# A recurrence and a two-layer network in one kernel: 20 of 24 chunks computed in pairs of two batches on 64x64 parts of the array

## The chip, the cores and the metric

The kernel runs on one core of one Trainium2 chip. Its engines are TensorE (PE in the profile, with PEld for its weight loads), VectorE (DVE), ScalarE (ACT), GpSimd (POOL) and SyncE (SP), which issues nearly all DMAs. The metric is the device time of one execution in microseconds, as a median of several runs; lower is better.

## The reference

`r`, `k`, `v`, `w` have the shape (batch 4, heads 8, tokens 768, 48). For every batch and head a 48x48 state is carried over the tokens, and the result of all heads of a token, 384 numbers, goes through two matrices with a leaky ReLU between them:

```python
for t in range(S):
    cur = einsum('bhd,bhe->bhde', u[None] * k_t, v_t)
    y[:, :, t] = einsum('bhd,bhde->bhe', r_t, state + cur)
    state = w_t[:, :, :, None] * state + einsum('bhd,bhe->bhde', k_t, v_t)
x = y.transpose(0, 2, 1, 3).reshape(B * S, H * D)     # 3072 x 384
h = x @ w_in                                          # 384 x 2048
out = maximum(0.01 * h, h) @ w_out                    # 2048 x 384
```

All inputs and the output are float32.

## The kernel before, in words

The tokens are cut into chunks of 128, six to a batch, 24 in all. Within a chunk the recurrence is written as matrix products: with L the running sum of ln w, `r*exp(L)` and `k*exp(-L)` are formed, transposed, and multiplied into scores of 128x128 tokens per head; the scores are masked to earlier tokens and multiplied with v (L829, "intra"); r times the state that came in is added (L824, "inter"); the state is brought forward with k and v (L798, "sums"). The part of the token itself, with u, is made on GpSimd and VectorE ("bonus", L435 to L447) and added to y (L478). y is transposed into `xT` and feeds the network: "up" (L901) multiplies with w_in into a PSUM tile `hp`, ScalarE applies Prelu (L916) into `g`, "down" (L928) multiplies with w_out into `op`, the result is copied (L939, L941) and stored (L945).

Chunks are done in the order `seq`. The first four come as two calls of `pair`: each takes 256 tokens of one batch, two neighbouring tokens to a partition (index j), and multiplies on parts of the array: its scores (L624) on 64x64 parts, its state sums (L583) and its intra product (L649) on 64x128 parts. The other 20 go through `single`, one chunk of 128 tokens at a time with the full array, except that the scores (L858) use 48 rows of two row halves for the two heads of a pair. `run` puts the scores of two chunks into one step for the chunks in MERGED. The transposes of r and k go over TensorE (L416) or, for chunks in RK_DMA, by a DMA transpose on SP's queue (L764); those of y over TensorE (L464) or, for Y_DMA, by a DMA transpose (L843).

The order of all work is made by `Plan`. Every step has a cost for each engine that may run it, a priority, the steps that it depends on and the buffers that it takes. `order` is a list scheduler over these costs: whenever an engine is free it takes the ready step with the lowest priority number whose buffers are free. Attention steps have ten times the chunk's number, ups and downs 1000 and more, so attention goes first and the network fills in. The instructions are then issued in that order, and each engine keeps it: an instruction that waits holds up all behind it on its engine. RANK and FORCE move priorities of the first 144 steps and fix the engine of some; SLACK adds a reserve to the planned end of steps from priority 50 on, LATE to DMAs. LEAD and AHEAD tie the first step (Ln) and the loads of a chunk to earlier chunks. `blocks` says how many chunks go through the network together. All PSUM tiles, eight of 512 columns, are one pool `ps`, with limits by kind (two `hp`, two `op`, one `cp`, one `ek`, two `yy`). Until 24 us gaps on TensorE are filled with products of zeros (L970).

Of the kernel before, what the change touches and what calls it, by code (L numbers as in the profile page):

```python
# [15 lines left out]
class Buf:  # L16


    def __init__(self, pool, kind=None):
        self.pool, self.kind, self.users, self.t, self.free_at = pool, kind or pool, [], None, 0.0  # L20


class Plan:
# [7 lines left out]
    def __init__(self, limits, slack_from, slack, late):  # L31
        self.steps, self.limits, self.late = [], limits, late
        self.slack_from, self.slack = slack_from, slack
# [8 lines left out]
    def order(self, pools):  # L42
# [10 lines left out]
        remain = {k: len(b.users) for k, b in bufs.items()}  # L53
        free_tiles = {p: [(0.0, k) for k in range(len(t))] for p, t in pools.items()}
        in_use = {}
        ready_at = [0.0] * n
        self.start, self.done, self.eng = [None] * n, [0.0] * n, [None] * n
# [15 lines left out]
        while events:  # L73
# [13 lines left out]
            for e in self.ENGINES:  # L87
# [3 lines left out]
                while ready[e]:  # L91
# [3 lines left out]
                    want, ok = {}, True  # L95
                    for b in self.steps[i][5]:
                        if b.t is None:
                            want[b.pool] = want.get(b.pool, 0) + 1
                            if in_use.get(b.kind, 0) >= self.limits.get(b.kind, 99):
                                ok = False  # L100
                    for p, k in want.items():
                        if sum(f <= now + 1e-9 for f, _ in free_tiles[p]) < k:
                            ok = False
# [10 lines left out]
                for b in takes:  # L114
                    if b.t is None:
                        slots = free_tiles[b.pool]
                        s = min(slots)
                        slots.remove(s)
                        b.slot = s[1]
                        b.t = pools[b.pool][s[1]]  # L120
                        in_use[b.kind] = in_use.get(b.kind, 0) + 1
                d = engs[e]
                self.start[i], self.eng[i] = now, e
# [7 lines left out]
                else:  # L131
# [5 lines left out]
                    self.done[i] = dma_free + lat + (self.late if now > 20 else 0.0)  # L137
                heapq.heappush(events, (free[e], 1, e, -1))
# [5 lines left out]
                for b in {id(b): b for b in (*reads, *takes)}.values():  # L144
                    b.free_at = max(b.free_at, self.done[i])
                    remain[id(b)] -= sum(u == i for u in b.users)
                    if remain[id(b)] == 0:
                        free_tiles[b.pool].append((b.free_at, b.slot))
# [7 lines left out]
BOTH = (1.5, 64, 1.45, 0.2)  # L156
WEIGHT = (2.08, 24, 2.6, 0.2)
# [4 lines left out]
RANK = {0: 15.37, 1: 14.4, 2: 3.33, 3: 23.03, 4: 38.76, 5: 12.01, 6: -26.8, 7: -21.87, 8: -21.96, 9: -19.05,  # L162
# [22 lines left out]
def kernel(  # L185
# [91 lines left out]
    with tc.manual_schedule():  # L277
# [10 lines left out]
        for t in pools["lw"]:  # L288
            nc.vector.memset(t[:, :, D:64], 0.0)
# [715 lines left out]
```

## Time and profile before

| | us |
|---|---|
| median of 3 runs (lowest to highest) | 182.65 (181.78 to 183.76) |
| the profiled execution, its own time | 181.38 |
| its span, first to last instruction | 179.6 |
| TensorE busy | 171.6 (2036 matmuls) |
| VectorE, ScalarE, GpSimd busy | 115.0, 115.3, 102.5 |
| up (L901), 720 matmuls, busy | 73.3 |
| down (L928), 384 matmuls, busy | 73.4 |
| first up | at 19.0 |

The granted clock of TensorE is 0.996 of full speed over the span. In lines of groups the columns are: line, engine, operation, what is written and read, shapes, count, then busy us and mean ns of one, then the idle time ahead. In lines of a timeline: start, us from the first start to the last end of the group, engine, line, what, count. Matmuls overlap, so the time that a group holds TensorE is read from its start to the start of the next group, not from the mean. In lines of waits: who waited for whom, us in total, how often, the longest.

### The profile page before, as it was taken

Reading aid. Unit: us, or ns where it says so; the run is one execution under the profiler, and the core shown is the slowest. Engines: PE = TensorE matmul, PEld = TensorE weight load, DVE = VectorE, ACT = ScalarE, POOL = GpSimd, SP = SyncE. Lnnn points to the kernel's source line nnn. Section 1 sums busy time; section 2 is a strip of 40 time slices with the busy share of each in tenths; the row PEclk is TensorE's granted clock in tenths of the full one; section 3 lists DMA queues with packets and bytes.
Section 4 is the critical chain, followed back from the end, with each engine's and each line's share of the span. In section 5 each row is a group of like instructions: output and inputs, shape, how many; then the busy total and the mean of one; then the engine's idle time right before and its main releaser. Section 6 shows DMA issues by size and latency. Waiting matters only on the chain.

```text
span 179.6 us, 5197 instructions
## 1 busy us (share of the span) xinstructions
PE 171.6 (96%) x2036; PEld 129.8 (72%) x2037; DVE 115.0 (64%) x231; ACT 115.3 (64%) x253; POOL 102.5 (57%) x138
## 2 busy tenths in 40 slices
PE   7798999999999999999999999999999999999991
PEld 2466888867778788877788767787788786787850
DVE  7699764289789898559677558397468297241102
ACT  2678968855867788884489774485486664652610
POOL 5999632574897686877469854667165665100000
PEclk9999999999999999999999999999999999999998
DMA  5999999998999999999999989999899996600112
GB/s 141 261 283 316 370 376 364 187 199 199 231 191 224 180 229 134 184 213 173 185 181 223 212 179 223 153 215 175 152 254 170 220 163 134 167 9 19 47 44 88
DMA packets 116571, 34.43 MB, mean 192 GB/s; under 512 B 109121, under 2 KB 115778, under 8 KB 116546
## 3 DMA queue, kind: packets, MB, share of 16 engines
q1 hardware_dynamic: 116544, 34.09, 95.8%
q8 instruction: 16, 0.26, 0.7%
q14 instruction: 9, 0.07, 0.1%
q10 hardware_dynamic: 2, 0.00, 0.0%
HBM read 25.17 MB, written 4.72 MB: 166 GB/s over the span
## 4 chain that ended last, share of the span: by engine, by line
PE 77%; DMA 11%; DVE 4%; ACT 2%; issue 2%; SPq 1%; POOL 0%; DVEq 0%; ACTq 0%
PE ps L901 35%; PE ps L928 28%; DMA in<-in_r_dram 3%; DMA in<-in_v_dram 3%; DMA in<-in_w_dram 2%; PE ps L858 2%; DMA xT<-y 2%; PE ps L829 2%; PE ps L717 2%; PE ps L824 2%; PE ps L416 2%; DVE rk L405 2%; PE ps L798 1%; PE ps L464 1%; DVE m L636 1%
## 5 line engine op out<-in xcount | busy, mean ns | idle before, releaser
L901 PE MATMUL ps<-xT,w_in_b 128*128 128x256 bf16 (+1 forms) x720 | 73.3, 251 | 0.4 <-ACT xT L471 0.2
L928 PE MATMUL ps<-w_out_b,g 128*128 128x384 bf16 x384 | 73.4, 326 | 0.0
L916 ACT ACTIVATE g<-ps 128x512 bf16<-128x512 f32 x96 | 56.8, 597 | 25.4 <-PE ps L901 23.2
L901 PEld LDWEIGHTS <-w_in_b 128*128 128x128 bf16 x720 | 57.8, 98 | 9.9 <-issue 0.7
L928 PEld LDWEIGHTS <-g 128*128 128x128 bf16 x384 | 35.2, 98 | 17.3
L405 DVE TENSOR_TENSOR rk<-in,ps 128x384 bf16<-128x384 f32 x46 | 24.5, 548 | 9.9 <-ACT ps L743 6.5
L435 POOL TENSOR_TENSOR ru<-in,ub 128x384 f32<-128x384 f32 x24 | 23.9, 1001 | 9.6 <-DMA in<-in_k_dram 7.6
L788 DVE TENSOR_TENSOR m<-ps,maskb 128x512 bf16<-128x512 f32 x40 | 25.1, 683 | 5.3 <-PE ps L858 5.3
L439 POOL TENSOR_TENSOR ru<-ru,in 128x384 f32<-128x384 f32 x24 | 24.6, 1027 | 3.0 <-DMA in<-in_r_dram 2.4
L775 POOL TENSOR_TENSOR sb<-s,a 128x384 bf16<-128x384 f32 x18 | 15.0, 831 | 16.8 <-ACT a L738 16.8
L447 POOL TENSOR_TENSOR vs<-in,dg 128x384 f32<-128x384 f32 x20 | 16.6, 830 | 9.1 <-DVE dg L443 8.4
L729 DVE TENSOR_TENSOR ci<-ps,lw 128x384 f32<-128x384 f32 x20 | 11.1, 555 | 9.7 <-PE ps L720 4.5
L939 DVE COPY o<-ps 128x384 f32<-128x384 f32 x10 | 5.6, 555 | 15.6 <-PE ps L928 15.4
L443 DVE TENSOR_REDUCE dg<-ru 128x8 f32<-128x384 f32 x24 | 12.9, 544 | 2.1 <-POOL ru L439 2.1
L478 DVE TENSOR_TENSOR y<-ps,vs 128x384 bf16<-128x384 f32 x20 | 11.1, 553 | 3.2 <-PE ps L829 2.6
L455 POOL CAST vb<-in 128x384 bf16<-128x384 f32 x24 | 12.0, 504 | 1.5 <-DMA in<-in_v_dram 1.4
L711 ACT ACTIVATE lw<-in 128x384 bf16<-128x384 f32 x20 | 10.4, 522 | 2.9 <-DMA in<-in_w_dram 2.9
L743 ACT ACTIVATE ps<-ps 128x384 f32<-128x384 f32 x20 | 9.6, 481 | 4.1 <-DVE ci L729 3.6
L738 ACT ACTIVATE a<-ps 64x4 f32<-64x4 f32 x36 | 6.0, 167 | 7.7 <-DVE ci L729 5.1
L813 DVE TENSOR_TENSOR s<-ps,sb 128x384 f32<-128x384 f32 x14 | 7.7, 552 | 3.8 <-PE ps L798 2.7
L747 ACT ACTIVATE ps<-ci 128x384 f32<-128x384 f32 x20 | 9.8, 491 | 0.0
L941 ACT COPY o<-ps 128x384 f32<-128x384 f32 x14 | 6.7, 479 | 4.2 <-PE ps L928 4.0
(90 smaller groups left out, 176.2 us busy)
## 6 DMA issues: line engine op xcount, KB each, us to landing
out_dram<-o SPq DMA_DIRECT2D x24, 192.0 KB, 3.7
in<-in_w_dram SPq DMA_DIRECT2D x20, 192.0 KB, 4.2
in<-in_k_dram SPq DMA_DIRECT2D x20, 192.0 KB, 4.2
in<-in_r_dram SPq DMA_DIRECT2D x20, 192.0 KB, 4.0
in<-in_v_dram SPq DMA_DIRECT2D x20, 192.0 KB, 4.0
in<-in_moe_w_out_dram SPq DMA_DIRECT2D x4, 768.0 KB, 12.1
in<-in_moe_w_in_dram SPq DMA_DIRECT2D x4, 384.0 KB, 6.8
in<-in_moe_w_in_dram SPq DMA_DIRECT2D x2, 768.0 KB, 9.0
```

Source lines behind the costliest of these rows:

```text
L405: (nc.gpsimd if e == "POOL" else nc.vector).tensor_tensor(out=o, in0=x, in1=i, op=ALU.mult)
L435: lambda e: nc.gpsimd.tensor_tensor(out=ru.t[:], in0=kv(), in1=ubv, op=ALU.mult),
L439: lambda e: nc.gpsimd.tensor_tensor(out=ru.t[:], in0=ru.t[:], in1=rv(), op=ALU.mult),
L443: lambda e: nc.vector.tensor_reduce(out=dg.t[:], in_=ru.t[:], axis=AX.X, op=ALU.add),
L447: lambda e: nc.gpsimd.tensor_tensor(out=vs.t[:], in0=vv(), in1=dg.t[:].unsqueeze(2).to_broadcast([128, H, D]), op=ALU.mult),
L455: {"POOL": 0.56}, lambda e: nc.gpsimd.tensor_copy(out=vb.t[:], in_=vv()),
L478: lambda e: nc.vector.tensor_tensor(out=y.t[:], in0=heads(yp.t), in1=vs.t[:], op=ALU.add),
L775: lambda e: nc.gpsimd.tensor_tensor(out=sb.t[:].rearrange("p g a d -> p (g a) d"), in0=s_in.t[:].rearrange("p g a d -> p (g a) d"), in1=a_ ...
L788: lambda e, par=par: nc.vector.tensor_tensor(out=m.t[:, par, :, :], in0=sc[par].t[:].rearrange("p (g t) -> p g t", g=NP), in1=maskb[:].uns ...
L901: nc.tensor.matmul(hp.t[:, a * N : (a + 1) * N], lhsT=w_in_b[:, t, (j + a) * 128 : (j + a + 1) * 128], rhs=xT[:, t, c0 : c0 + N], start=(a ...
L916: lambda e, hp=hp, g=g, j=j, J=J, N=N: nc.scalar.activation(out=g.t[:, j : j + J, 0:N], in_=hp.t[:, 0 : J * N].rearrange("p (a n) -> p a n ...
L928: nc.tensor.matmul(op.t[:, 0:DM], lhsT=g.t[:, j, off : off + 128], rhs=w_out_b[:, j, :], start=(j == 0), stop=(j == NJ - 1))
```

## The change

`single` and `run` go; `late(n)` takes their place and treats chunks n and n+1 together, which are now the same 128 tokens of two batches b and b+1. Batch x sits on partitions 64x to 64x+63, with two neighbouring tokens (j) to a partition. A load moves 64 partitions with 96 floats in a row. Each of the scores, the inter and the intra product and the state sums is then a set of matmuls on 64x64 parts: a row half for the batch or the head's parity, a column half for the batch, the token parity or the head's parity. They are laid in two rows on TensorE: first half of inter and the scores (`row(behind, scores)`), and, after the masks, the other half of inter, intra and the sums (`row(ahead, intra, sums)`). The state holds head pairs as 128x192 instead of 128x384. `seq` is arranged in pairs of batches.

With it: ci is two VectorE subtractions and additions from one cumulative sum; a bonus product `vs` is written in 64-partition pieces (four a pair); the last of the r products in `pair` (tokens of the first parity) may go to GpSimd (cost 1.15 on VectorE, 1.0 on GpSimd) and stands there in the program's order for both pairs; a new mask `maskp` is made by eight selects on GpSimd at the start, and maskb goes. Prelu puts the tokens back in order by reading PSUM with a stride. The last chunk's down is cut into columns 0 to 255 and 256 to 383. The up steps of one-chunk blocks wait for all of the w_in columns that they read. `blocks` has eight single chunks (six before). The planner also holds off a step whose PSUM tile is still in use by the other side, and can hand out neighbouring tiles together. RANK and FORCE are empty, LEAD is 5, AHEAD 3, SLACK 0, LATE 0.6; DMA transposes now carry a pair, for r and k 16 blocks instead of 8, for y 6 instead of 3. `pair` is split into part lists, of which only the whole one is used, and its state is kept in two halves of 64 partitions.

Instructions in program order: matmuls 2037 before, 3106 after, of which on 64x64 parts 64 and 1568; GpSimd selects 8 and 15; vs 20 and 40; loads in the late chunks 80 and 80; DMA transposes 21 and 16.

```diff
-RANK = {0: 15.37, 1: 14.4, ...
-FORCE = {23: "DVE", 26: "DVE", ...
+RANK = {}
+FORCE = {}
-    RK_DMA = {6, 11, 12, 14, 15, 16, 17, 18, 19, 20, 21, 22, 23}
-    Y_DMA = {8, 10, 16, 17, 20, 21, 22, 23}
-    MERGED = {6, 10, 12, 14, 16, 18, 20}
-    LEAD = 4
-    AHEAD = 4
-    SLACK_FROM = 50
-    SLACK = 0.2
-    LATE = 0.0
+    RK_DMA = {8, 10, 12, 14, 16, 18, 20, 22}
+    Y_DMA = {8, 10, 12, 14, 16, 18, 20, 22}
+    LIMITS = {"hp": 2, "op": 2, "cp": 1, "ek": 3, "yy": 2, "warm": 1, "warm2": 1}
+    LAST = [(0, 256), (256, DM)]
+    LEAD = 5
+    AHEAD = 3
+    SLACK_FROM = 60
+    SLACK = 0.0
+    LATE = 0.6
-    blocks = [2, 1, 1, 1, 1, 2, 2, 2, 2, 2, 1, 1, 2, 2, 2]
+    blocks = [1, 1, 1, 1, 1, 1, 2, 2, 2, 2, 2, 2, 2, 2, 1, 1]
...
+        for q in (0, 64):
+            for js in range(2):
+                for j in range(2):
+                    nc.gpsimd.affine_select(
+                        out=maskp[q : q + 64, js, j, :], in_=maskp[q : q + 64, js, j, :], compare_op=ALU.is_gt, fill=0.0,
+                        base=j - js, pattern=[[2, 64]], channel_multiplier=-2,
+                    )
...
+                        {"DVE": 0.75 + 0.4 * wide, "POOL": 0.1 + 0.9 * wide} if bank is er0 else {"DVE": 0.15 + 0.4 * wide},
...
+        def late(n):
...
+                            out=Flat(slots[name]).t.rearrange("p (h f) -> p h f", h=H)[64 * x : 64 * x + 64],
+                            in_=src[b + x, :, t0 : t0 + L, :].rearrange("h (p j) d -> p h (j d)", j=2))
...
+            def scores(e):
+                for js in range(2):
+                    for g in range(NP):
+                        for par in range(2):
+                            q0 = 64 * par
+                            for x in range(2):
+                                q = slice(64 * x, 64 * x + 64)
+                                nc.tensor.matmul(
+                                    scs[js][par].t[q, g * 128 : (g + 1) * 128].rearrange("p (j t) -> p j t", j=2),
+                                    lhsT=rkT2.t[q0 : q0 + D, js, NP + g, q], rhs=rkT2.t[q0 : q0 + D, :, g, q],
+                                    start=True, stop=True, skip_group_check=True)
+
+            def sums(e):
+                for g in range(NP):
+                    for js in range(2):
+                        for x in range(len(pps)):
+                            q = slice(64 * x, 64 * x + 64)
+                            for par in range(2):
+                                nc.tensor.matmul(
+                                    pps[x].t[64 * par : 64 * par + 64, g * D : (g + 1) * D],
+                                    lhsT=rk2.t[q, js, 1, 2 * g + par, :], rhs=vbs[js].t[q, 2 * g + par, :],
+                                    start=(g == 0 and js == 0), stop=(js == 1), skip_group_check=True)
+
+            def summed(x, j, cols, **k):
+                nc.tensor.matmul(
+                    yps[x].t[64 * j : 64 * j + 64, cols], start=(x, j) not in begun, stop=True, skip_group_check=True, **k)
+                begun.add((x, j))
+
+            def inter(flip):
+                for g in range(NP):
+                    for x in range(2):
+                        par = x ^ flip
+                        q0, h = 64 * par, 2 * g + par
+                        for j in range(2):
+                            summed(x, j, slice(h * D, (h + 1) * D),
+                                   lhsT=rkT2.t[q0 : q0 + D, j, g, 64 * x : 64 * x + 64], rhs=sbs[x].t[q0 : q0 + D, g, :])
+
+            def intra(e):
+                for h in range(H):
+                    for js in range(2):
+                        for x in range(2):
+                            q = slice(64 * x, 64 * x + 64)
+                            for j in range(2):
+                                summed(x, j, slice(h * D, (h + 1) * D), lhsT=ms[js].t[q, h % 2, h // 2, 64 * j : 64 * j + 64],
+                                       rhs=vbs[js].t[q, h, :])
...
+            s_sc = step(
+                {"PE": 0.65 if first else 0.75}, row(behind, scores), P0 + 1, deps=[*s_T, *s_sbs], reads=[rkT2, *sbs],
+                takes=[sc for js in range(2) for sc in scs[js]] + ([] if first else yps))
...
+            s_yi = step(
+                {"PE": 0.6 + 0.1 * (not first) + 0.2 * (not last)}, row(ahead, intra, *([] if last else [sums])), P0 + 2,
+                deps=[*s_ms, *s_vbs, *s_T, *s_sbs, s_rk[1, 0], s_rk[1, 1]], reads=[*ms, *vbs, rk2, rkT2, *sbs],
+                takes=[*yps, *pps])
...
-                    deps=[s for ch in chs for s in xt_steps[ch]] + win_s[j // 2 : (j + J) // 2])
+                    deps=[s for ch in chs for s in xt_steps[ch]] + win_s[j // 2 : (j + J + 1) // 2])
+                def leaky(e, hp=hp, g=g, j=j, J=J, N=N, c0=c0):
...
+                        i = i.rearrange("p (a x t) -> p a t x", x=2, t=64) if N == L else i.rearrange("p (s x t) -> p s t x", x=2, t=64)
+                        o = o.rearrange("p a (t x) -> p a t x", x=2) if N == L else o.rearrange("p a (s t x) -> p (a s) t x", x=2, t=64)
+                    nc.scalar.activation(out=o, in_=i, func=AF.Prelu, alpha=0.01)
...
+                for x, (d0, d1) in enumerate(LAST if ch == NCH - 1 else [(0, DM)]):
```

More of the change, by code (lines that the diff above doesn't have):

```diff
@@ L642, in pair @@
[L642 to L652 removed]
+            s_keep = []
@@ L664, in add_vs @@
+            s_y1 = step(
+                {"PE": 0.19}, inter, P0 + 1, deps=[s_sb, *(s for x in s_T for s in x)], reads=[rkTb, sb], takes=yps)
             def add_vs(e):
@@ L753, in single @@
[L753 to L762 removed]
+                        heads(c1.t), lhsT=mat[:], rhs=lw.t[:, j, :, 0:D], start=(j == 0), stop=(j == 1),
@@ L833, in single @@
[L833 to L841 removed]
+                        nc.vector.tensor_tensor(out=sx.t[:], in0=part(pps[x].t), in1=sbs[x].t[:], op=ALU.add)
```

848 lines of the change are left out of this document (465 added, 383 removed), and 16 rows, old and new, of the table RANK.

## The prediction

> **What bounds the kernel now.** I read the page first (shares and slices), then the groups of TensorE by shape, its timeline in the steady stretch, the timelines of the start (TensorE and GpSimd), and last TensorE's waits.
>
> ```profile
> span 179.6 us, 5197 instructions
> PE 171.6 (96%) x2036; PEld 129.8 (72%) x2037; DVE 115.0 (64%) x231; ACT 115.3 (64%) x253; POOL 102.5 (57%) x138
> PE   7798999999999999999999999999999999999991
> DMA  5999999998999999999999989999899996600112
> ```
>
> TensorE is full from the fourth slice to the last but one, and no other engine is over 64%. So the time is the sum of TensorE's work, plus what the start leaves idle, plus a tail. The chain of waits says the same: 77% of it is TensorE. DMA is busy too, but nothing on TensorE waits for it there:
>
> ```profile
> PE ps L416 <- DVE rk L405: 0.5, 1, 0.5
> PE ps L717 <- ACT lw L711: 0.2, 1, 0.2
> PE ps L901 <- ACT xT L471: 0.2, 1, 0.2
> ```
>
> All waits of TensorE together are 3.6 us; two, of 0.2 us each (L717 on lw, L901 on xT), stand behind 26 us. A microsecond of TensorE work taken out is a microsecond won, if the new order waits as little.
>
> **The rates.** A group's mean ns is a latency; the rate is read from starts.
>
> ```profile
> 105.61 0.81 PE L928 MATMUL ps<-w_out_b,g 128*128 128x384 bf16 x4
> 106.36 0.62 PE L858 MATMUL ps<-rkT 48*128 48x128 bf16 x16
> 106.91 0.82 PE L928 MATMUL ps<-w_out_b,g 128*128 128x384 bf16 x4
> 107.57 1.47 PE L901 MATMUL ps<-xT,w_in_b 128*128 128x256 bf16 x12
> ```
>
> The second L928 group takes 107.57-106.91 = 0.66 for 4, 0.162 each. L901 with 256 columns goes on to 108.88: 0.109 each; with 128 columns, 24 in 1.34 (chain, 25.88 to 27.22): 0.056. L858, two row halves side by side, steps by (0.62-0.22)/15 = 0.027, half of 0.056, so 16 take 0.45; but the next group starts 0.55 after it: leaving its part size costs some 0.09. Before it, L928 takes 0.75 instead of 0.65: entering costs 0.095. A visit to another part size is thus 0.19. Likewise L829 (48 columns, full array) is 0.025 each, L824 and L798 (96 columns) 0.042, L720 (1 column) 0.026.
>
> ```profile
> 10.86 0.64 PE L624 MATMUL ps<-rkT 48*64 48x128 bf16 x32
> 11.43 0.50 PE L970 MATMUL ps<-zeros 128*128 128x512 bf16 x3
> 21.28 0.64 PE L583 MATMUL ps<-vb,rk 64*128 64x96 bf16 x16
> 21.75 0.58 PE L649 MATMUL ps<-vb,m 64*128 64x48 bf16 x32
> ```
>
> L624 already runs on 64x64 parts: (0.64-0.22)/31 = 0.0136 a matmul of 128 columns, and four of them make 0.055, one full-array matmul of that length. So four parts do run at once. L649 has two row halves and 48 columns: (0.58-0.18)/31 = 0.0129, twice that is 0.026, the rate of one L829.
>
> **The change, part by part.** Counts are from the order of both programs.
>
> *Small products of chunks 5 to 24.* Before: scores 160 x 0.028 = 4.5, 13 visits x 0.19 = 2.4, intra 160 x 0.025 = 4.0, inter 72 x 0.042 = 3.1, state sums 64 x 0.042 = 2.7; 16.7 us. After: scores 320 x 0.0136 = 4.4, 20 visits (two rows a pair) 3.7, and 640 + 288 + 256 = 1184 matmuls of 48 columns on 64x64 parts. No row has that shape. Lower bound: four of them in the 0.025 of one L829, 0.0063 each, 7.4 us. Upper: the column halves give nothing and they go as L649, 0.0129, 15.3 us; beyond that, one after the other as L829, 30 us. I take 0.0072 (8.5 us), near L624, where four parts overlap. The weight loads say why it is not quite 0.0063: L624's loads, 64 columns, are 106 ns, L649's, 128 columns, 93; L624's matmuls run from 213 to 240 ns, the long ones where the load had not come ahead, so a load alone holds a part some 27 ns, and four times 0.0072 is 0.029, just over that. After: 16.6 us. The four-fold split thus only pays for itself.
>
> The Trainium skill, "TensorEngine Tiling (Array Packing)", section Instruction Overhead, speaks against this split: each matmul carries some 60 cycles, so a dimension already small should not be tiled for, and here the moving side is 48. By that rule, taken for the engine as a whole, the small products would stay at the rate of L829 and the sum would end 21 us higher, by mine it ends at the one below. L649 shows that two row halves share the floor; no run here shows it for column halves.
>
> *What goes for certain.* Transposes of r and k: 56 to 32 (pairs at 4 and 6 stay on TensorE, the others go by DMA), of y in these chunks 36 to 12: 48 x 0.056 = -2.7. Totals 80 for 72: +0.2. The cumulative sums stay 20 x 0.162. Blocks of one chunk, 8 for 6: up 96 x 0.056 for 48 x 0.109, +0.1; the last chunk's down in two column parts, +0.1.
> TensorE: 16.6-16.7-2.7+0.2+0.2 = **-2.4 us** (bounds -3.5 and +4.4 by the two rates).
>
> *The start.* GpSimd stood thus before:
>
> ```profile
> 3.65 1.39 POOL L312 TENSOR_SCALAR_AFFINE_SELECT mask<-mask 64x256 bf16<-64x256 bf16 x2
> 5.09 0.86 POOL L312 TENSOR_SCALAR_AFFINE_SELECT spread<-spread 64x256 bf16<-64x256 bf16 x2
> 6.00 0.19 POOL L317 MEMSET a<- 128x8 f32 x3
> 6.28 1.96 POOL L435 TENSOR_TENSOR ru<-in,ub 128x384 f32<-128x384 f32 x2
> ...
> 17.04 0.82 POOL L357 CAST w_in_b<-in 128x768 bf16<-128x768 f32 x1
> ```
>
> It had no gap between the selects and its first product, so anything put in front is late one to one. Now eight selects of 64x64 for maskp come in front, each between the memset of that size (0.15) and a 128x128 select (0.29), less maskb and two memsets: some +1.1, first product at 7.4. It also gets the last r product of pairs 0 and 2 from VectorE, 1.0 each by L435. In the new order then stand, ahead of its two casts of w_in (columns 512 to 1023), four L435 (0.96 apart), four L439 (0.94), the two r products, four L455 (0.46) and two L447 (0.79): 3.8+3.8+2.0+1.8+1.6 = 13.0, so casts from 20.4 to 22.0. The second up step, now of 512 columns, needs both, and behind it on TensorE stand pair 2's intra and all later ups. Before, ups had 4.8 us by 26 us (first at 19.0); after, about 2.7: **+2.1 us** (0, if the weights' landing holds it anyway, to 4, if the first up slips to 20 as well). RANK and FORCE, which moved steps of this stretch, are empty now, so nothing puts the casts ahead.
>
> *Waits in the steady stretch.* Between the scores of the first late pair and its second row stand 2.6 us of ups and downs; four masks need 0.2 + 3 x 0.6 (their spacing) + 0.68 = 2.7. The second row of chunks 8 and 9 and their up are 6.6 us apart, against 1.3 for two y and a DMA transpose of 3.7 to 4.9 us for half the columns, some 5.5 to 7. The first row takes six PSUM tiles at once, leaving two for up and down. SLACK went from 0.2 to 0. Against that, each late load moves 384 B a packet instead of 192 (28 against 19 ns in the trace), which eases DMA by (81920 x 19 - 40960 x 28)/16 = 25 us, more than the transposes' third more work. I take **+1.2** (0 to 6).
>
> *Hidden.* vs on GpSimd: 40 of 64 partitions for 20, at 0.83 the same each, +17 us; the compact states give 7 back; GpSimd comes to 8.7 us in a pair whose ups and downs alone take 10.5. ScalarE loses 14 us (Ln, a, xT, rkT, o). Prelu now reads PSUM with a stride in 80 of 96: at 0.6 nothing, at 0.9 +24 us on ScalarE, still under 75%. If such cover went, a tile of up would come free 0.3 late each time.
>
> *Tail.* The last copy is 128 columns instead of 384: **-0.3**.
>
> Sum: -2.4+2.1+1.2-0.3 = +0.6 on the profiled execution's 181.4 (span 179.6 and 1.8 around it), 182.0. That execution lies 1.3 below the median of the runs, 182.65, so **183.2 us** as a median: no change, where about 1% (1.8 us) can be told.
>
> **The rivals.** *Column halves don't overlap at 48 columns* (the split doesn't do what it says): 1184 x (0.0129-0.0072) = +6.7, **190 us**. For it: the load is longer than the 20 ns of streaming, where L624 hid it behind 53. Against: in L624 all four loads run side by side. It decides from 0.0095 a matmul (+2.7). 0.20. *The floor is one for the engine*: each of the 1184 takes the 0.025 of a lone L829, +21, **204 us**; L649 at half of that speaks against, though its runs are only 32 long and the new second row is 112. 0.06. This is the case that the skill's 60 cycles would make. *The second row waits*: masks or banks hold each pair 0.5 us more, +5, **188 us**; for: six tiles at once, no slack; against: VectorE at 64%, and most later pairs have 3.9 us between the rows. 0.15. *Faster*: casts in time (0), no waits (0), 0.0063: -3.5-0.3, **179 us**; for: DMA eased, TensorE the only bound; against: the count of GpSimd's work. 0.21. The forecast has 0.38.
>
> **How the numbers follow.** Faster by over 1% is the faster case but for its upper edge, and a little of the forecast: 0.22. Slower is the three slower rivals (0.41) and the upper edge of the forecast: 0.46. Within 1%: 0.32. Range 179.2 to 192: it leaves out the 204 and the edges. The forecast's own range is 181 to 186.
>
> **What will show it.** L923 and L917 in a row: 0.029 for four is right, over 0.038 the first rival. Second up step at 22 us and a TensorE gap on GpSimd's w_in cast before it; none would make the start wrong. TensorE's waits behind 26 us about 1 us; 5 us would be the third rival. Visits other than 0.19 would move the sum 0.2 for each 0.01.

## The result and the profile after

| | before | after |
|---|---|---|
| median of the runs (lowest to highest), us | 183.08 (181.78 to 183.76) | 198.53 (198.12 to 199.45) |
| span of the profiled execution | 179.6 | 196.8 |
| ratio, 95% interval | | 1.086 [1.079, 1.094] |

The change makes the kernel 15 us slower. Medians here and below are over all executions of a kernel; ratios leave out an execution that lies over 1.5% above the fastest of its kernel. The head of the page after, its slices, the queue that carries nearly all transfers, and the chain of waits by engine; behind them the queue and the chain of before:

```profile
span 196.8 us, 7320 instructions
PE 174.4 (89%) x3102; PEld 129.5 (66%) x3106; DVE 110.6 (56%) x235; ACT 105.2 (53%) x206; POOL 112.5 (57%) x162
...
PE   6878999699599885979879978869999999999993
...
DMA  6999999999999989989998999989998242111112
...
q1 hardware_dynamic: 81712, 35.66, 90.5%
...
PE 38%; DMA 29%; POOL 13%; SPq 5%; DVE 5%; issue 4%; ACT 2%; DVEq 0%; POOLq 0%; ACTq 0%
```

```profile
q1 hardware_dynamic: 116544, 34.09, 95.8%
...
PE 77%; DMA 11%; DVE 4%; ACT 2%; issue 2%; SPq 1%; POOL 0%; DVEq 0%; ACTq 0%
```

TensorE is busy for almost the same time, 174.4 for 171.6, but its row of nines is broken from slice 8 to slice 27. Transfers were 11% of the chain and are 29%. The transfers end at nearly the same time in both: the last load lands at 151.6 before and at 149.5 after. What differs is how much TensorE still has to do then: 28 us before, 47 after. Behind 26 us the profile puts TensorE's waits at 0.4 us before and 14.5 after; taken from start to start of its matmuls, waits of over 0.1 us sum to 3.1 us before and to 17.6 after.

The waits of after, for the two engines that take a load first and for TensorE (who waited for whom, us in total, times, longest); behind them GpSimd's line of before:

```profile
POOL ru L876 <- DMA in<-in_k_dram: 16.1, 5, 5.9
ACT lw L793 <- DMA in<-in_w_dram: 9.3, 6, 2.5
...
PE ps L806 <- ACT lw L793: 5.4, 4, 2.2
...
PE ps L1050 <- DVE y L1014: 2.0, 1, 2.0
...
PE ps L923 <- DMA rkT<-rk: 1.6, 1, 1.6
```

```profile
POOL ru L435 <- DMA in<-in_k_dram: 7.6, 12, 1.4
```

TensorE's largest wait, L806, is the cumulative sum waiting for Ln on ScalarE (L793), and Ln in turn waits for the load of w, 9.3 us in all; GpSimd waits 16.1 for k, twice as long as before. The chain of waits shows the same between 108 and 131 us (start, length, what):

```profile
108.51 5.46 DMA in<-in_w_dram
...
114.05 0.85 ACT lw L793
114.94 0.43 PE ps L806 x2
...
116.31 4.13 DMA in<-in_r_dram
...
120.54 1.03 DVE rk L457 x2
...
123.18 7.93 DMA rkT<-rk
```

A load, Ln, a sum, a load, the r product, a transpose: each step of a pair stands behind a transfer. TensorE's queue keeps the order that the planner wrote, so the ups and downs behind such a step wait too, though their data is there. That last clause was the theory to test.

How late the transfers are against the order can be told exactly, since the planner is part of the kernel and gives each step a date. Before, loads land within 1.8 us of their dates over the whole run. After, the first late load lands 3.2 us behind its date, the loads at 60 us are 7 behind, at 100 us 14, and the last one 21; from 140 us on every step of TensorE is 20 to 21.5 late. The planner's whole schedule ends at 174.5 us (177.2 for the kernel before). So 3 us of the lag come before 40 us, and the rest grows evenly, with the number of loads.

The planner prices a late load of 64 partitions (192 KB) at 0.75 us, half of the 1.5 of a load of 128 partitions and 384 KB. On the chip a late load that follows another lands 0.95 us behind it (median of 55 such pairs). For 80 loads that is 80 x 0.2 = 16 us, of the 18 by which the lag grows. In the kernel before, the price is 1.1 and the landings are 1.03 apart (49 pairs).

### The profile page after: what moved, and what is told of

The parts are those of the page before. It is cut to its first block, busy times and chain, and to the rows that moved or that the text cites. A ratio compares the mean times of both kernels' runs of the same rounds, so it can differ in the third digit from the quotient of the medians.

```text
span 196.8 us, 7320 instructions
## 1 busy us (share of the span) xinstructions
PE 174.4 (89%) x3102; PEld 129.5 (66%) x3106; DVE 110.6 (56%) x235; ACT 105.2 (53%) x206; POOL 112.5 (57%) x162
## 4 chain that ended last, share of the span: by engine, by line
PE 38%; DMA 29%; POOL 13%; SPq 5%; DVE 5%; issue 4%; ACT 2%; DVEq 0%; POOLq 0%; ACTq 0%
PE ps L1081 16%; PE ps L1050 15%; DMA in<-in_w_dram 8%; DMA in<-in_moe_w_out_dram 6%; SPq L780 5%; DMA in<-in_r_dram 5%; DMA rkT<-rk 4%; DMA in<-in_k_dram 3%; PE ps L923 3%; DMA xT<-y 3%; POOL vs L890 3%; DVE rk L457 2%; POOL ru L489 2%; POOL vb L509 1%; ACT lw L793 1%
## 5 line engine op out<-in xcount | busy, mean ns | idle before, releaser
L1050 PE MATMUL ps<-xT,w_in_b 128*128 128x128 bf16 (+1 forms) x768 | 76.7, 246 | 3.4 <-DVE y L1014 2.0
L1081 PE MATMUL ps<-w_out_b,g 128*128 128x384 bf16 (+2 forms) x400 | 76.2, 320 | 0.3 <-DVE w_out_b L412 0.3
L890 POOL TENSOR_TENSOR vs<-in,dg 64x384 f32<-64x384 f32 x40 | 33.0, 824 | 2.7 <-DVE y L1014 0.8
L981 DVE TENSOR_TENSOR m<-ps,maskp 128x512 bf16<-128x512 f32 x40 | 24.8, 683 | 8.9 <-PE ps L906 8.5
L876 POOL TENSOR_TENSOR ru<-in,ub 128x384 f32<-128x384 f32 x20 | 19.8, 1000 | 16.2 <-DMA in<-in_k_dram 16.1
L1092 DVE COPY o<-ps 128x384 f32<-128x384 f32 (+2 forms) x17 | 9.1, 533 | 31.3 <-PE ps L1081 22.0
L509 POOL CAST vb<-in 128x384 bf16<-128x384 f32 x24 | 11.5, 505 | 16.6 <-PE ps L917 13.6
L793 ACT ACTIVATE lw<-in 128x768 bf16<-128x768 f32 x10 | 8.4, 841 | 9.3 <-DMA in<-in_w_dram 9.3
L884 DVE TENSOR_REDUCE dg<-ru 128x8 f32<-128x384 f32 x20 | 10.7, 547 | 4.7 <-POOL ru L880 4.7
L961 POOL TENSOR_TENSOR sb<-s,a 128x192 bf16<-128x192 f32 x18 | 8.8, 506 | 1.9 <-ACT a L820 1.4
L923 PE MATMUL ps<-vb,m 64*64 64x48 bf16 x640 | 7.5, 187 | 1.8 <-issue 1.8
L923 PE MATMUL ps<-sb,rkT 48*64 48x48 bf16 x288 | 6.2, 192 | 3.0 <-DMA rkT<-rk 1.6
L1126 PE MATMUL ps<-zeros 128*128 128x128 bf16 (+1 forms) x33 | 6.9, 329 | 1.9 <-DVE zeros L326 1.7
```

What stands on the lines that cost most here:

```text
L509: {"POOL": 0.56}, lambda e: nc.gpsimd.tensor_copy(out=vb.t[:], in_=vv()),
L793: lambda e: nc.scalar.activation(out=lw.t[:, :, :, 0:D].rearrange("p j h d -> p h j d"), in_=Flat(slots["w"]).t.rearrange("p (h j d) -> p ...
L876: lambda e, ru=ru, j=j: nc.gpsimd.tensor_tensor(out=ru.t[:], in0=view("k", j)(), in1=ubv, op=ALU.mult),
L884: lambda e, ru=ru, dg=dg: nc.vector.tensor_reduce(out=dg.t[:], in_=ru.t[:], axis=AX.X, op=ALU.add),
L890: lambda e, x=x, j=j, q=q, dg=dg: nc.gpsimd.tensor_tensor(out=vs2[x].t[64 * j : 64 * j + 64], in0=view("v", j)()[q], in1=dg.t[q].unsqueeze ...
L923: nc.tensor.matmul(yps[x].t[64 * j : 64 * j + 64, cols], start=(x, j) not in begun, stop=True, skip_group_check=True, **k)
```

## The experiments

Theory A: the order is frozen with a wrong price, and that is all. B: the transfers are the bound in any order. C: GpSimd, with 33 us of vs products, is late and holds the loads' buffers. Ratios are to runs of the kernel before on the same chip, whose median was 181.4 to 183.2 us from one chip to the next. So a gain between runs on different chips is read from the two ratios, one hundredth being 1.8 us.

### Prices alone, in both kernels

Changed kernel, two prices:

```diff
-PART = (0.75, 32, 1.45, 0.2)
+PART = (0.88, 32, 1.45, 0.2)
-TRK2 = (2.9, 128, 0.9, -0.6)
+TRK2 = (3.4, 128, 0.9, -0.6)
```

> Only two prices that the order is planned with are changed: a late load of 192 KB from 0.75 us of the queue to 0.88 (they landed 0.89 us apart on average between 36 and 150 us, the transposes and stores in between taken off), a transpose of 2048 columns from 2.9 to 3.4 (they land 3.3 to 3.9 us behind the load before them). Theory A, the frozen order: TensorE's order was written for loads that end at 128 us, they end at 149.5, so TensorE stands at attention steps whose data is late while ups and downs that could run are queued behind them; with the right prices most of the 16 us of new waits go: 181 to 187 us. Theory B, the transfers are the bound in any order (80 loads, 16 transposes and the stores fill the queue to 150 us): no gain, over 195. Theory C, GpSimd (33 us of vs products) is late and holds the loads' buffers: no gain, over 195.

Measured: 192.85 us, ratio 1.060 [1.053, 1.067]. Faster than after by 4.8 us, but between the theories.

The kernel before, one price:

```diff
-LOAD = (1.1, 64, 1.4, 0.2)
+LOAD = (0.75, 64, 1.4, 0.2)
```

> The kernel before with the same mistake put into it: its price of a late load goes from 1.1 us to 0.75, nothing else. Theory A: its loads land some 1.05 us apart (36.9 to 151.6 us for the last 76, with stores and transposes between), so its TensorE order runs ahead of the data by some 15 us at the end and TensorE waits: 189 to 198 us. Theories B and C: the work on every engine and queue is the same, so 181 to 185 us, as before.

Measured: 198.73 us, ratio 1.094 [1.085, 1.102]. No instruction was added, and the kernel before loses 17 us. Two lines of its page, and then three of its waits:

```profile
span 197.5 us, 5202 instructions
PE 175.8 (89%) x2037; PEld 130.6 (66%) x2037; DVE 117.4 (59%) x234; ACT 115.3 (58%) x250; POOL 102.1 (52%) x138
```

```profile
POOL ru L435 <- DMA in<-in_k_dram: 14.8, 12, 3.3
...
PE ps L858 <- DMA rkT<-rk: 4.0, 3, 1.6
...
PE ps L901 <- DMA xT<-y: 2.7, 1, 2.7
```

89% of TensorE and 14.8 us of GpSimd's waits for k are the picture of the changed kernel. Its loads end 19 us behind their dates. RANK and FORCE of that kernel were set for the order at 1.1, so part of the 17 us may be their loss of fit. The planned end shows none (176.3 us at 0.75, 177.2 at 1.1); the lag of the loads is there in any case.

At 0.93 (`LOAD = (0.93, ...)`):

> The kernel before with its late load priced at 0.93 instead of 1.1; by themselves such loads landed 0.94 apart, with transposes and stores between them some 1.05. Price 0.75 cost it 17 us. If what counts is the margin against the pace with everything in between: about half of that lag, 186 to 192 us. If the price of the load alone, without the rest, is what the order needs: 181 to 184.

Measured: 192.12 us, ratio 1.059 [1.053, 1.066]: a slope. For 0.17 off the price, 0.10 below the 1.03 at which loads land, it loses 11 us, and for 0.35 off it 17.

All prices of the changed kernel mended (`PART` 0.93, `TRK2` 3.5, `TY2` 1.7, `BEGIN` of GpSimd 7.9, the second row 0.72 to 1.10, intra ahead of inter in it):

> All prices of the order as measured: a late load 0.93, the transposes 3.5 and 1.7, the second row of small products 0.72 to 1.10 (112 x 0.0079 and a visit of 0.19), GpSimd free from 7.9 us; the second row issues its intra products ahead of its inter products. Theory A (all of the loss is the order): 183 to 188 us. Theory B' (the order is half of it, the transfers the other half: a pair's eight loads, transposes and two stores take some 14.3 us of the queue, about what TensorE needs for a pair): 189 to 194, like the 192.9 with two prices mended.

Measured: 194.57 us, ratio 1.074 [1.068, 1.081]. Just above the case called B' there, and far from A. Right prices alone do not bring the kernel back: planned with them, the schedule itself ends at 183.3 instead of 174.5, and the run is 7 to 8 us behind that.

### GpSimd

```diff
-out=vs2[x].t[64 * j : 64 * j + 64], in0=view("v", j)()[q],
+out=vs2[x].t[64 * j : 64 * j + 64, 0:1], in0=view("v", j)()[q, 0:1],
```

> Order as in the changed kernel; the 40 vs products on GpSimd cover one head instead of eight (the bonus of late chunks is wrong), which takes some 25 us off GpSimd. Theories A and B: nothing to gain, 196 to 200 us. Theory C: buffers come free earlier, loads follow, under 190.

Measured: 197.92 us, ratio 1.090 [1.085, 1.095]. Its page, groups of GpSimd:

```profile
L890 POOL TENSOR_TENSOR vs<-in,dg 64x48 f32<-64x48 f32 x40 | 10.5, 264 | 3.7 <-DVE y L1014 1.5
L876 POOL TENSOR_TENSOR ru<-in,ub 128x384 f32<-128x384 f32 x20 | 19.9, 1002 | 24.4 <-DMA in<-in_k_dram 24.4
```

vs takes 10.5 us instead of 33.0, and the gain is spent waiting for k: 24.4 us instead of 16.1. Theory C falls.

### Lighter loads in the unchanged order

```diff
-in_=src[b + x, :, t0 : t0 + L, :].rearrange("h (p j) d -> p h (j d)", j=2))
+in_=src[b + x].rearrange("h s d -> (h s d)")[t0 * DM : (t0 + L) * DM].rearrange("(p f) -> p f", p=64))
```

> Order and every instruction as in the changed kernel, but each late load fetches its 192 KB as 64 runs of 3072 bytes instead of 512 of 384, so heads and tokens are mixed up. The weights' 768 KB in runs of 1536 bytes landed 2.07 us apart, 0.52 per 192 KB, so the loads should land well inside the 0.75 us that the order was planned with. Theories A and B: the lag of the loads is gone and so are TensorE's waits behind 40 us: 179 to 185 us. Theory C: GpSimd's work is the same, so little changes, over 193.

Measured: 186.54 us, ratio 1.028 [1.023, 1.033]. The same order, the same instructions on every engine, and by the ratios 10.6 us are back. A late load behind another lands 0.81 us after it instead of 0.95: 80 x 0.14 = 11.

The transfers by themselves:

```python
for i in range(12): both(i)         # 128 partitions, 8 x 384 B each, 384 KB
for i in reversed(range(12)): wide(i)      # 128 partitions, 8 x 192 B, as the late loads before
for i in range(12): part(i, i % 2)  # 64 partitions, 8 x 384 B, halves in turn, as after
for i in reversed(range(12)): part(i, 0)   # the same, low half only
for i in range(12): long(i, i % 2)  # 64 partitions, 3072 B in a run
...                                 # halves in turn on two queues; transposes; stores
```

> Transfers by themselves on an idle core, twelve in a row of each kind, read from the distance of their landings; no arithmetic, the outputs are zeros. Two chunks of one batch on 128 partitions (384 KB, 384 bytes a packet): 1.50 us as at the start of both kernels, 0.75 per 192 KB. One chunk on 128 partitions with 192 bytes a packet, the kernel before's late load: 0.84. One chunk on 64 partitions with 384 bytes, the changed kernel's late load: 0.89 if the half width itself is what made the planned 0.75 wrong; 0.75 if it is the contention with transposes and stores. The same on one half of the partitions only, and on two queues in turn: the same or worse. Runs of 3072 bytes: 0.5. Transposes of 2048 columns: 2.9 alone, against 3.3 to 3.9 seen beside other transfers; stores 0.6.

Stretch by stretch, in that order but without the two queues (us, DVE and GpSimd busy, clock, DMA share, GB/s):

```profile
5.20:17.30 12.10, 0.00 (x0) 0.00 (x0) 1.00 1.13 313
21.30:30.30 9.00, 0.00 (x0) 0.00 (x0) 1.00 1.00 196
34.90:43.30 8.40, 0.00 (x0) 0.00 (x0) 1.00 1.20 224
47.10:55.60 8.50, 0.00 (x0) 0.00 (x0) 1.00 1.21 173
60.10:68.00 7.90, 0.00 (x0) 0.00 (x0) 1.00 0.87 214
81.30:93.70 12.40, 0.00 (x0) 0.00 (x0) 1.00 1.09 216
94.70:106.50 11.80, 0.00 (x0) 0.00 (x0) 1.00 0.96 348
```

By their landings: full width 0.60 us per 192 KB (0.75 expected), 192-byte packets 0.94, halves in turn 0.87, low half only 1.04, long runs 0.81 (not 0.5), transposes 2.48, stores 0.54; two queues in turn 0.92, no gain. So 384-byte packets are worth 36% of a load at full width (0.94 to 0.60), and on half width most of that is lost again. It is the width, not contention: nothing else ran. Beside other transfers, in the changed kernel, the 0.87 becomes 0.95.

The Trainium skill, "SBUF — State Buffer", section "Door 1: The DMA port swizzle", states that the partition number's highest bit picks one of two sets of 8 ports, so that partitions 0 to 63 reach 8 of 16. That agrees with 173 against 313 GB/s for the low half. The 224 GB/s of halves in turn lie between the two; that neighbouring transfers overlap there in part is a reading that no run shows.

Then the full width in the changed kernel, one load where the second half-width load stood:

```diff
+if x == 1:
+    t = min(t0, S - 2 * L)
     nc.sync.dma_start(
-        out=...[64 * x : 64 * x + 64], in_=src[b + x, :, t0 : t0 + L, :]...
+        out=..., in_=src[b, :, t : t + 2 * L, :].rearrange("h (p j) d -> p h (j d)", j=2))
```

> Order as in the changed kernel; each pair of late loads of 64 partitions is one load of 128 partitions with the same 384-byte packets, issued where the second one stood. So that one transfer can do it, it takes two chunks of one batch instead of one of two, and late chunks compute on other tokens than they should. By themselves such loads landed 1.20 us apart for 384 KB, against 1.68 for two of 64 partitions. Theory W (the half width is the cause: it makes the planned 0.75 per 192 KB wrong): the lag of the loads goes and with it 10 to 13 us, 185 to 189 us, as with the long packets. Theory X (the number of packets, or the transposes of 2048 columns, hold the queue): as many packets as before, so 195 to 199.

Measured: 187.87 us, ratio 1.028 [1.023, 1.033]. The last load lands at 138.8 instead of 149.5: 10.7 us earlier, and the kernel is 10.7 us faster. Its page, and its waits of TensorE:

```profile
span 185.3 us, 7249 instructions
PE 173.0 (93%) x3102; PEld 129.3 (70%) x3106; DVE 110.2 (59%) x235; ACT 105.1 (57%) x206; POOL 112.6 (61%) x162
```

```profile
PE ps L925 <- issue: 2.5, 3, 1.2
...
PE ps L1052 <- DVE dg L886: 1.6, 1, 1.6
```

Theory W, that the width does it, is shown: no wait of TensorE for a load or for Ln is left among its longest, with the number and size of the packets, the transposes and GpSimd as they were. The run also has 40 late loads instead of 80, but their number does not set the 0.95: stores of 192 KB at full width followed each other every 0.54 us. Long runs had brought the same 10.6 us at half width: what costs the time is the pace against the price, and the half width is what puts 384-byte packets behind it.

### The last five microseconds

With full-width loads and the other prices mended:

> Full-width loads (late chunks on other tokens than they should), a load left at the price of 0.75 that is now about right, and the other prices as measured: transposes 3.5 and 1.7, second rows 0.72 to 1.10, GpSimd free from 7.9 us; intra ahead of inter in the second row. If the last 5 us over the kernel before are these prices: 180 to 184 us. If they are work and latency that the change added: 185 to 189, as with the full-width loads alone.

Measured: 188.97 us (185.77 to 189.81), too wide apart for a ratio. One execution, at a granted clock of 1.000, took 185.77, and three, at 0.991, took 188.9 to 189.8. None lies in the first case, but the one is 2.1 us under the median with full-width loads alone. So these prices are not all of the 5 us; whether they are worth 2 us stays open. Full-width loads put into the order of the run with all prices mended:

> The order of the run with all prices mended (a load at 0.93), with full-width loads put into it (late chunks on other tokens than they should). If that order is limited by the transfers themselves (theory B'): the loads now come earlier than planned and TensorE moves up where the order allows it, 183 to 188 us against 194.6. If the order itself is worse than the unchanged one, or waits elsewhere: over 190.

Measured: 189.95 us, ratio 1.037 [1.032, 1.042]. Between the two cases. TensorE stays within 3.4 us of its dates, so this order, ending at 183.3 by its own plan, is itself the slower one; the same loads in the unchanged order gave 187.9. Long packets with all other prices mended and a load at 0.60:

> Long runs of 3072 bytes (heads and tokens mixed up) and all other prices as measured, a load at 0.60. With the loads out of the way, if the 5 us by which the same order with long packets still stood over the kernel before are false prices too (start of GpSimd, second rows): 180 to 184 us. If they are work that the change added (start, small products, instruction fetch): 185 to 188.

Measured: 195.48 us, ratio 1.073 [1.066, 1.080]; neither case. 0.60 was my own wrong price: these loads land 0.81 apart in the unchanged order and 0.76 here, and the loss is again what a price 0.2 too low costs.

Without the selects of maskp (the block of eight `affine_select` left out):

> As the run with full-width loads in the unchanged order, but without the eight selects that make maskp (it stays all ones), so GpSimd begins its products 1.7 us earlier. If the start term of the prediction is right (GpSimd late one to one, 2.1 us in all with the two r products): 1 to 2 us faster than that run. If the weights' landing holds the start anyway: the same within 0.5.

Measured: 187.03 us, ratio 1.024 [1.019, 1.029]; the interval overlaps that of the full-width run. Up to 33 us TensorE is 1.0 us ahead of that run, at 39 us 0.2 and at 72 us no longer: what the start gives is lost again before then.

r and k of every other late pair back on TensorE (`RK_DMA = {10, 14, 18, 22}`, mended prices):

> As the run with all prices mended, but r and k of every other late pair are transposed on TensorE again, which takes 4 x 3.4 = 14 us off the transfers and puts 64 transposes (3.6 us) on TensorE. Theory A: 1 to 4 us slower than the run with all prices mended. Theory B': 2 to 5 us faster than it.

Measured: 200.71 us, ratio 1.105 [1.101, 1.110]. Slower by more than either case. The granted clock is not the reason: it was 0.971 over the profiled span, but the execution at 0.998 took 200.16 us, the shortest of the four. TensorE has two stops there that wait for nothing the profile shows, 4.7 us together, against one of 0.7 with all prices mended. So the run tells nothing sure of the transposes.

TensorE's rows told more. A second row without a stop, and one with (timeline of after):

```profile
74.33 0.31 PE L923 MATMUL ps<-sb,rkT 48*64 48x48 bf16 x16
74.48 0.71 PE L923 MATMUL ps<-vb,m 64*64 64x48 bf16 x64
75.01 0.45 PE L917 MATMUL ps<-vb,rk 64*64 64x48 bf16 x32
75.39 0.83 PE L1050 MATMUL ps<-xT,w_in_b 128*128 128x256 bf16 x6
99.47 0.31 PE L923 MATMUL ps<-sb,rkT 48*64 48x48 bf16 x16
99.62 0.38 PE L923 MATMUL ps<-vb,m 64*64 64x48 bf16 x25
101.25 0.50 PE L923 MATMUL ps<-vb,m 64*64 64x48 bf16 x39 [1.26 <-issue]
101.57 0.44 PE L917 MATMUL ps<-vb,rk 64*64 64x48 bf16 x32
101.94 0.34 PE L806 MATMUL ps<-lw,tstr 128*128 128x384 bf16 x1
```

112 matmuls take 75.39-74.33 = 1.06 us in the one and 2.47 in the other. "issue" means that TensorE waited for nothing that the profile shows. Such stops inside the ten second rows sum to 2.5 us in after (three of them) and to 2.7 with full-width loads (four). In first rows there are others, but those wait for rk on VectorE. To see whether the rows are too dense, half of the late intra products were left out of the full-width version:

```diff
-for js in range(2):
+for js in range(1):
```

> Full-width loads in the unchanged order (late chunks on other tokens than they should), and the intra products of late chunks for the first of the two tokens only: 320 matmuls of 48 columns and as many weight loads less. At the 0.0079 us that they take in an undisturbed row that is 2.5 us of TensorE. If TensorE also runs out of instructions in these rows (three stops of 0.3 to 1.2 us marked as issue, 2.5 us, in the run with full-width loads): 4 to 5 us less than its 187.9, 183 to 184. If those stops have another cause: 185 to 186.

Measured: 183.60 us, ratio 1.009 [1.006, 1.012]. By the ratios that is 3.4 us below the full-width run (187.87 came from a chip on which the kernel before took 183.22, 183.60 from one on which it took 181.89), between the two cases: the time alone does not decide. The traces do. The ten second rows take 13.3 us together with full width and 8.2 here; 2.6 of the 5.1 are the 320 matmuls, at the 0.0082 that one takes in a row without a stop, and the rest went with the stops, of which one, of 0.77 us, is left. Some of it is lost again in first rows, which wait 1.1 us for rk.

The column split undone for intra in the full-width version (one matmul on all 128 columns for two), which also puts intra behind the state sums in the row:

```diff
-for j in range(2):
-    summed(x, j, ..., lhsT=ms[js].t[q, h % 2, h // 2, 64 * j : 64 * j + 64], rhs=vbs[js].t[q, h, :])
+nc.tensor.matmul(yps[x].t[:, h * D : (h + 1) * D], ..., lhsT=ms[js].t[q, h % 2, h // 2, :], rhs=vbs[js].t[q, h, :])
```

> Full-width loads in the unchanged order (late chunks on other tokens than they should); the intra products on two row halves with all 128 columns, 320 matmuls instead of 640, the column split undone for them. At 0.0129 against twice 0.0079 they take 4.1 us instead of 5.1, and one more change of part size in each second row gives 1 to 2 back: 187 to 188.5 by the work alone. If TensorE runs out of instructions in the long rows: 185 to 186.5, with fewer stops marked as issue.

Measured: 185.50 us, ratio 1.018 [1.012, 1.025]. By the ratios that is 1.7 us below the full-width run, with intervals that touch: again between the cases. A second row of it:

```profile
102.75 0.31 PE L925 MATMUL ps<-sb,rkT 48*64 48x48 bf16 x16
102.90 0.42 PE L919 MATMUL ps<-vb,rk 64*64 64x48 bf16 x32
103.25 0.57 PE L943 MATMUL ps<-vb,m 64*128 64x48 bf16 x32
103.75 0.34 PE L808 MATMUL ps<-lw,tstr 128*128 128x384 bf16 x1
```

80 matmuls in 1.00 us, and none of its second rows has a stop: together they take 9.5 us instead of 13.3. Ten rows at 1.00 instead of 1.06 give 0.6 of that, the rest are the stops. In exchange first rows wait 2.5 us for rk, and one stop of 0.8 marked issue stands just behind a second row.

That the supply of instructions causes the stops is the likeliest reading. Instructions come in blocks of 16 KB (24 of them after and with full width, 22 in the runs with fewer products, 16 before). In the traces of the changed kernel and its 15 variants TensorE has 32 stops of over 0.15 us marked issue behind 26 us, the longest of 2.96, and every one ends 1.2 to 1.7 us behind the end of such a block's transfer; moments that near behind a block are about 6% of the time. The kernel before and its two repriced versions, with 16 blocks, have none. Not all stops are in small products: five are in ups and downs. So the stops go with the blocks; why some blocks come too late and most do not, no run shows, since none changed the blocks alone.

The transposes as plain copies, with full-width and with half-width loads:

```diff
-nc.sync.dma_start_transpose(
+nc.sync.dma_start(
     out=rkT2.t.rearrange("p x g t -> p (x g) t"), ...
```

> Full-width loads in the unchanged order (late chunks on other tokens than they should), and the eight transposes of r and k by transfer are plain copies of the same 512 KB, so late chunks compute with r and k not transposed. The transposes held SyncE's queue for 4.2 us each and took 2.5 us of transfers alone. If they are what keeps that run 5 us over the kernel before: 183 to 185. If not: 187 to 188.5.

> The changed kernel with its half-width loads, the eight transposes of r and k replaced by plain copies (r and k of late chunks not transposed). Theory W (half-width loads come 0.84 to 0.95 apart against 0.75 planned): the copies take back only what they save themselves, 8 x 2 us at most, of which the lag of the loads gives back half or so: 189 to 195. If the transposes are the real cause: under 187.

Measured: 183.70 us, ratio 1.008 [1.006, 1.011], and 195.18, ratio 1.069 [1.061, 1.076]. By the ratios the copies win 3.5 us with full width and 3.2 with half width, and there the loads still land 0.95 apart: the transposes are the second user of the same transfers, not the cause. With full width, second rows take 11.1 us instead of 13.3, so some 2 us of the gain are again fewer stops.

Whole columns and the first two mended prices together:

> The two repairs that leave the result whole, together: the prices of the first experiment (a late load 0.88, the large transpose 3.4) and the intra products on all 128 columns. The prices alone gave 192.9, the columns alone took 2.4 us off the full-width run. If both add up: 189 to 191.5. If the half-width loads set the pace anyway and the columns only lengthen a wait: 192 to 194. It does not reach the kernel before (181 to 183) in either case, since the loads still end at 150 us and are planned too early.

Measured: 190.56 us, ratio 1.050 [1.044, 1.055]. They add up (1.060 for the prices, less the 0.009 that the columns gave, is 1.051). No version of the changed kernel with its own loads reached the kernel before.

## Why the prediction was wrong, point by point

**The step that failed: waits in the steady stretch, +1.2 (0 to 6).** They grew by 14.5 us (3.1 to 17.6), and that is nearly all of the miss. Behind the term stands one step: that wide packets ease the transfers by 25 us, more than the transposes add, so that TensorE would go on waiting for no load. It took 28 ns a packet from the early loads, which have all 128 partitions, and left out that the new loads have 64. In after a packet of a late load takes 33 ns, which eases the transfers by 11 us, not 25; and the packets of the transposes take 31 ns instead of 26 and are a third more, which adds 17.5 us where as many more at the old price would have added 10. So the queue's time rose, from 0.958 x 179.6 = 172 to 0.905 x 196.8 = 178 us. More than that, the order was written for loads 0.75 apart where they land 0.95 apart, and so it ran ever further ahead of its data: with the pace mended and the order kept, 10.6 us came back twice. "DMA is busy too, but nothing on TensorE waits for it" was true only while the order held to the transfers' pace; with the kernel before at 1.1 a load it did, by a small margin. Some 5 us stay over the kernel before with full-width loads. Plain copies for the transposes win 3.5 of them and the stops marked issue are 2.7, partly the same; how the rest divides stays open.

**"The time is the sum of TensorE's work."** True of before, because its order was planned with transfer prices that the chip keeps. The price of a load stood in the diff's surroundings (0.75 beside 1.5 for twice the bytes) and was never set against a landing.

**Small products.** 0.0072 forecast, 0.0082 in a row without a stop (95 steps in 0.78 us), under the 0.0095 from which the first rival decides. With scores and 20 visits that makes some 18.5 us where 16.6 were forecast. The second rival, 0.025 for the engine as a whole, was wrong: four parts run at once. The Trainium skill, "TensorEngine Tiling (Array Packing)", section Instruction Overhead, states some 60 cycles for each matmul. Here that is no floor for the engine as a whole: one part takes a matmul every 0.033 us, four parts together one every 0.0082. What no case forecast are the stops inside the rows, 2.5 us in after.

**Visits.** 0.19 forecast; 0.095 in and 0.095 out, also for these parts.

**Transposes.** -2.7 forecast; from start to start L416 and L464 took 7.9 us and their heirs L468 and L518 6.0: -1.9.

**The start.** +2.1 forecast, about 1.0 measured, and by another way. TensorE's first ups, and GpSimd's two casts of w_in:

```profile
21.09 1.50 PE L1050 MATMUL ps<-xT,w_in_b 128*128 128x128 bf16 x24
22.52 0.59 PE L724 MATMUL ps<-vb,m 64*128 64x48 bf16 x32
23.28 1.50 PE L1050 MATMUL ps<-xT,w_in_b 128*128 128x128 bf16 x24 [0.16 <-ACT g L1070]
```

```profile
20.96 1.59 POOL L410 CAST w_in_b<-in 128x768 bf16<-128x768 f32 x2
```

The casts came nearly when forecast (20.4 to 22.0), but the sign named for them, a gap of TensorE on the cast, is not there: the ups of columns 512 to 1023 stand at 23.28, 0.7 us behind the casts, and the 0.16 ahead of them is put down to g. What moved is the first up, from 19.0 to 21.1; just ahead of it, from 19.2 to 20.8, ScalarE has two casts of w_in. Ups by 26 us are 3.2 us. Before they were 36 matmuls of 256 columns and a few more, 4.2 us from start to start and not 4.8, which adds up spans that run into the next group. That little of the cost reaches the end is shown by the run without selects, which starts 1.0 us earlier and gains at most 0.8.

**Hidden work.** Right. GpSimd is at 57%, its vs products cost nothing, and Prelu with a stride takes 598 ns as against 597.

**Rivals.** The third (the second row waits, 188 us) was right that the waits come in the steady stretch and wrong on the cause: not masks or banks, but loads that come late for Ln and for the products. No case had late loads.

## What to carry to other kernels

Where an order is written from prices, a price 0.1 to 0.2 us too low per load is not a small error (it cost some 11 us in either kernel here): set each price against the landings in a trace, with all that shares the queue, before reading TensorE's share as the bound. Price a transfer by rows with the same number of partitions, not by packet size alone: two transfers on 64 partitions are not one on 128. A split that doubles the instructions of a row is not free: stops of TensorE on issue came with it.

## What the runs showed of the hardware, not expected

- Loads of 192 KB by themselves: 0.60 us at full width, 0.87 with halves in turn, 1.04 on one half (313, 224 and 173 GB/s), with 384-byte packets in all three.
- Runs of 3072 bytes on 64 partitions in turn land only a little faster (0.81) than eight runs of 384 do (0.87).
- A transpose of 2048 columns held SyncE's queue for 4.2 us (median) beside other transfers and 2.7 alone; those of r and k before, half as large, held it 1.9.
- TensorE stopped for 0.2 to 1.3 us, marked as issue, inside second rows of 224 instructions (matmuls and their weight loads) in 1 us, in 8 of 21 such rows (after, full width, copies); in rows of 160 instructions in 2 of 21 (half of intra, whole columns alone and with the two prices). All 32 stops on issue behind 26 us, in the changed kernel and its variants, end 1.2 to 1.7 us behind the end of a 16 KB block of instructions.
- The granted clock over the span differs between executions of one kernel, and here the time did not follow it: the changed kernel took 198.12 us at 0.980 and 198.47 at 1.000. In the kernel before with loads at 0.75 it was 0.982 to 0.991 in all four executions, 0.91 between 40 and 80 us in the profiled one, where the kernel before had 0.995 and more. No run was made on why.
